# Moving 32 tile transposes from TensorE to the DMA crossbar in a fused attention and MLP kernel

## The chip, the cores and the metric

The kernel runs on one core of one Trainium2 chip. The metric is the device time of one execution in microseconds (us). Most executions of one kernel agree within a per cent or so; a run counts as slow when it is over 1.5% above the fastest of its kernel. The kernel before ran again in every round of experiments (medians 234.05, 234.35, 234.15 and 233.81); the kernel after did not, so an experiment is compared with it by their ratios to the kernel before. Ratios quoted with an interval are the mean time of one kernel's fast runs over the mean of the other's fast runs of the same rounds, with a 95% interval, so they are not quite the ratio of the medians quoted beside them.

Engines: PE is TensorE, PEld its weight loads, DVE is VectorE, ACT is ScalarE, POOL is GpSimd, SP is SyncE, which here does nothing but issue DMAs; "SPq" is SP's DMA queue.

## The reference, cut to what matters

```python
B, S, D, H, F = 1, 2048, 448, 16, 1792        # head size 28, bf16
x  = A_x
xn = layernorm(x)
# branch A: linear attention with a softmax feature map
qkv = xn @ wqkv
phi_q = concat(softmax(q @ w_phi), softmax(-(q @ w_phi)))      # the same for k
o = (phi_q @ (phi_k.T @ v)) / (phi_q @ sum(phi_k) + 1e-6)
A = o @ wo
# branch B: token shift mixer and MLP on xn
x1 = xn + shift(gelu(layernorm(xn) @ w1)) @ w2
B_ = x1 + gelu(layernorm(x1) @ w3) @ w4
return x + A + B_
```

Tokens are cut in 16 tiles of 128. Two of the intermediate results come out with tokens on partitions, but are next needed with features on partitions: the scaled LN2 output `g_tok` (input of `w3`), and the attention output `o_tok` (input of `wo`). Each of these 32 tiles (128 tokens x 448 features, padded to 512) has to be transposed.

## The kernel before

The kernel has a loading and LN1 phase (0 to about 52 us), a k phase (52 to 95 us: k, v, q and the kv sums), and an output phase of four stages of four tiles each (95 us to the end). A helper records all instructions, works out the semaphores, and plays each engine's list in order; that is why most instructions carry the helper's line (L186 matmul, L190 transpose, L194 ACT, L198 elementwise, L201 or L204 DMA) and must be told apart by their tiles.

Buffers are reused under their first name. In the lines of the trace below, `xnT` in the output phase is `oT` and `o_tok`; `phik` there is `h3T` (gelu of the w3 product); `vaug` is the scratch of the attention division, the sums `xs` and the output buffer `outb`; `w` is any of w1, w2, w3, w4; `hi` holds the qk weights at the start, q features later.

The parts that the change and the argument touch:

```python
        def g_apply(i):
            ln_apply(pool, g_tok[:, i % 4, 0:D], xn[:, i, 0:D], rs2, i)

        def g_T(i, b):                                  # LN2 tile, b = banks[7] (banks[5] in the k phase)
            for kc in range(KC):
                R.tr(tview(b)[:, 128 * kc:128 * kc + 128], g_tok[:, i % 4, 128 * kc:128 * kc + 128], ident[:, :])
            j = 128 * (i % 4)
            R.ew(dve, "tensor_copy", gT[:, (i // 4) % 2, :, j:j + 128], tview(b).rearrange("p (c d) -> p c d", c=KC))

        def o_T(i):                                     # attention tile
            b = banks[7]
            for kc in range(KC):
                R.tr(tview(b)[:, 128 * kc:128 * kc + 128], o_tok[:, i % 4, 128 * kc:128 * kc + 128], ident[:, :])
            j = 128 * (i % 4)
            R.ew(dve, "tensor_copy", oT[:, (i // 4) % 2, :, j:j + 128], tview(b).rearrange("p (c d) -> p c d", c=KC))

        def fin_tile(i):
            g, j = divmod(i, 4)
            b = bank(3, 4)
            x_sum(i)                                    # POOL
            # ... 14 matmuls with w4, 4 with wo into b ...
            R.ew(dve, "tensor_tensor", outb[:, i % 4, :], b[:, 0:D], xs[:, i % 2, :], op=ALU.add)
            R.dma(out2d[128 * i:128 * i + 128, :], outb[:, i % 4, :])
# ...
        for g in range(NG):                             # the output phase: 14 w3 chunks per stage,
            fill = []                                   # with this work spread between them
            # ...
            for j in range(4):
                i = 4 * g + j
                fill.append(lambda i=i: num_tile(i))
                if g >= 1:
                    fill.append(lambda i=i - 4: fin_tile(i))
                if g < 2:
                    fill.append(lambda i=i + 8: w2_tile(i))
                    # ...
                if g + 1 < NG:
                    fill.append(lambda i=i + 4: g_T(i, banks[7]))
                if i > 0:
                    fill.append(lambda i=i - 1: o_T(i))
```

Note what is tied together: both transposes of a slot write bank 7, so the second cannot start until DVE has copied the first one out.

The softmax here doesn't subtract the row's maximum and nothing guards it: scores larger than these inputs give would overflow.

Of the kernel before, what the change touches and what calls it, by code (L numbers as in the profile page):

```python
# [17 lines left out]
class Recorder:  # L18
# [177 lines left out]
    def ew(self, eng, name, out, *args, **kw):  # L196
        aps = [v for v in list(args) + list(kw.values()) if hasattr(v, "tensor")]
        self.op(eng, lambda e: getattr(e, name)(out, *args, **kw), [out], aps)  # L198

    def dma(self, out, in_, eng="SP"):  # L200
        self.op(eng, lambda e: e.dma_start(out, in_), [out], [in_], dma=True)  # L201


def bass_parallel_sum__linear_kernel_hedgehog__mixer_s_mlp__prompt_kernel(  # L204
# [6 lines left out]
    NT, NG, KC, NC, NM, FC, HP = 16, 4, 4, 4, 4, 14, 32  # L211
# [6 lines left out]
    with es:  # L218
        R = Recorder(nc, es)
# [9 lines left out]
        def view(h, cols, dt=BF16, at=0):  # L229
            a = h[:, at // 2:at // 2 + cols * DTB[dt] // 2]  # L230
            return a if dt == BF16 else a.bitcast(dt)

        def new(name, cols, dt=BF16):
            return view(region(name, cols * DTB[dt]), cols, dt)

        banks = []
# [16 lines left out]
        gT = new("gT", 2 * KC * 512).rearrange("p (b c s) -> p b c s", b=2, c=KC)  # L253
# [16 lines left out]
        g_tok = new("g_tok", 4 * 512).rearrange("p (b d) -> p b d", b=4)  # L270
        kvq = new("kvq", 8 * 128).rearrange("p (b e) -> p b e", b=8)
        kvT = view(w1_r, NC * 224).rearrange("p (c f) -> p c f", c=NC)
        ident = new("ident", 128)
# [14 lines left out]
        oT = view(xnT_r, 2 * KC * 512).rearrange("p (b c s) -> p b c s", b=2, c=KC)  # L288
        o_tok = view(xnT_r, 4 * 512, at=2 * KC * 512 * 2).rearrange("p (b d) -> p b d", b=4)
# [21 lines left out]
        def bank(*ids):  # L311
            k = turn.get(ids, 0)
            turn[ids] = k + 1
            return banks[ids[k % len(ids)]]

        def tview(b, n=512, base=0):
            return b[:, :].bitcast(BF16)[:, base:base + n]

        dve, pool = "DVE", "POOL"
# [5 lines left out]
        def load_rows(dst, src):  # L325
# [31 lines left out]
                                             fill=0.0, base=0, channel_multiplier=1), [maskb[0:CR, :]], [maskb[0:CR, :]])  # L357
        R.op(pool, lambda e: e.affine_select(mb, mb, pattern=[[DH, 4], [0, DH]], compare_op=ALU.is_ge,
                                             fill=0.0, base=DH - 1, channel_multiplier=-1),
# [4 lines left out]
                                             fill=1.0, base=0, channel_multiplier=1), [rsel[0:DH, :]], [rsel[0:DH, :]])  # L364
# [16 lines left out]
        def ln_scale(mvt, rst, a, n):  # L381
            R.ew(pool, "tensor_scalar", rst[:, a:a + n, 2], mvt[:, a:a + n, 1], LN_EPS, 1.0, op0=ALU.add, op1=ALU.mult)
            R.ew(pool, "tensor_scalar", rst[:, a:a + n, 1], mvt[:, a:a + n, 0], -1.0, 0.0, op0=ALU.mult, op1=ALU.add)
            R.ew(pool, "tensor_tensor", rst[:, a:a + n, 0], rst[:, a:a + n, 2], mhalf[:, 0:n], op=ALU.pow)
# [51 lines left out]
        rot = [(0, 1, 2, 3, 4, 5)]  # L436

        def rot_b():
            return bank(*rot[0])

        def v_tile(i):
            b = rot_b()
            for kc in range(KC):
                R.mm(b[:, 0:D], xnT[:, kc, 128 * i:128 * i + 128], wv[:, kc, :], kc == 0, kc == KC - 1)
            R.ew(dve, "tensor_copy", vaug[:, i, :].rearrange("p (h e) -> p h e", e=HP)[:, :, 0:DH],
                 b[:, 0:D].rearrange("p (h e) -> p h e", e=DH))

        def k_tile(i):
            b = rot_b()
            for kc in range(KC):  # L450
                R.mm(b[:, 0:D], xnT[:, kc, 128 * i:128 * i + 128], wpk[:, kc, :], kc == 0, kc == KC - 1)
            R.act(phik[:, i, 0, :], b[:, 0:D], ACT.Exp)
            R.act(phik[:, i, 1, :], b[:, 0:D], ACT.Exp, scale=-1.0)
            ph = phik[:, i, :, :].rearrange("p s (h e) -> p (s h) e", e=DH)
            r = i % 4
            R.ew(dve, "tensor_reduce", ksum[:, r, :], ph, axis=AX.X, op=ALU.add)
            R.ew(dve, "reciprocal", rks[:, r, :], ksum[:, r, :])
            R.ew(pool, "tensor_tensor", ph, ph, rks[:, r, :].unsqueeze(2).to_broadcast([128, 2 * H, DH]), op=ALU.mult)

        def kv_tile(i):  # L460
            for c in range(NC):
                R.mm(banks[6 + c // 2][:, 224 * (c % 2):224 * (c % 2) + 224].rearrange("p (s f) -> p s f", s=2),
                     vaug[:, i, 128 * c:128 * c + 128], phik[:, i, :, CR * c:CR * c + CR],
                     i == 0 and c % 2 == 0, i == NT - 1)
# [23 lines left out]
        def w2_tile(i):  # L488
            b = rot_b()
            for m in range(NM):  # L490
                c0 = 2 + 128 * i - SHIFTS[m]
                R.mm(b[:, 0:D], hT[0:CR, m, c0:c0 + 128], w2[0:CR, m, :], m == 0, m == NM - 1)
            R.ew(dve, "tensor_tensor", xn[:, i, 0:D], b[:, 0:D], xn[:, i, 0:D], op=ALU.add)
            ln_stats(st2, mv2, xn, i)
# [1 line left out]
        def g_apply(i):  # L496
            ln_apply(pool, g_tok[:, i % 4, 0:D], xn[:, i, 0:D], rs2, i)

        def g_T(i, b):
            for kc in range(KC):  # L500
                R.tr(tview(b)[:, 128 * kc:128 * kc + 128], g_tok[:, i % 4, 128 * kc:128 * kc + 128], ident[:, :])
            j = 128 * (i % 4)
            R.ew(dve, "tensor_copy", gT[:, (i // 4) % 2, :, j:j + 128], tview(b).rearrange("p (c d) -> p c d", c=KC))

        def num_tile(i):
            g, j = divmod(i, 4)
# [17 lines left out]
                 q_n[:, r, :, 0:DH], rden.unsqueeze(2).to_broadcast([128, H, DH]), op=ALU.mult)  # L524

        def o_T(i):
            b = banks[7]
            for kc in range(KC):
                R.tr(tview(b)[:, 128 * kc:128 * kc + 128], o_tok[:, i % 4, 128 * kc:128 * kc + 128], ident[:, :])
            j = 128 * (i % 4)  # L530
            R.ew(dve, "tensor_copy", oT[:, (i // 4) % 2, :, j:j + 128], tview(b).rearrange("p (c d) -> p c d", c=KC))

        def w3_chunk(g, fc):
            b = bank(0, 1, 2)
# [4 lines left out]
        def x_sum(i):  # L539
            R.ew(pool, "tensor_tensor", xs[:, i % 2, :], xn[:, i, 0:D], xtok[:, i, :], op=ALU.add)  # L540

        def fin_tile(i):
            g, j = divmod(i, 4)
            b = bank(3, 4)
            x_sum(i)
            for fc in range(FC):
                R.mm(b[:, 0:D], h3T[:, g % 2, fc, 128 * j:128 * j + 128], w4[:, fc, :], fc == 0, False)
            for kc in range(KC):
                R.mm(b[:, 0:D], oT[:, g % 2, kc, 128 * j:128 * j + 128], wo[:, kc, :], False, kc == KC - 1)
            R.ew(dve, "tensor_tensor", outb[:, i % 4, :], b[:, 0:D], xs[:, i % 2, :], op=ALU.add)  # L550
            R.dma(out2d[128 * i:128 * i + 128, :], outb[:, i % 4, :])


# [30 lines left out]
        for i in range(NT + 2):  # L584
            if i < NT:
                k_tile(i)
            if i >= 2:
                kv_tile(i - 2)
            if i < NT:
                if i % 2 == 0:  # L590
                    v_tile(8 + i // 2)
                else:
                    w2_tile(i // 2)
                    if i % 8 == 7:
                        ln_scale(mv2, rs2, i // 2 - 3, 4)
                q_chunk(*divmod(i, 4))
                if i == 9:
                    for j in range(4):
                        g_apply(j)
                if i >= 12:  # L600
                    g_T(i - 12, banks[5])
                    rot[0] = (0, 1, 2, 3, 4)
        kv_copy()
        R.ew(pool, "memset", o_tok[:, :, D:512], 0.0)
        rot[0] = (3, 4)
        for g in range(NG):
            fill = []
            if g + 1 < NG:
                fill.append(lambda g=g: [g_apply(4 * g + 4 + j) for j in range(4)])
            if g == 0:  # L610
                fill.append(kv_blocks)
            for j in range(4):
                i = 4 * g + j
                fill.append(lambda i=i: num_tile(i))
                if g >= 1:
                    fill.append(lambda i=i - 4: fin_tile(i))
                if g < 2:
                    fill.append(lambda i=i + 8: w2_tile(i))
                    if j == 3:
                        fill.append(lambda i=4 * g + 8: ln_scale(mv2, rs2, i, 4))  # L620
                if g + 1 < NG:
                    fill.append(lambda i=i + 4: g_T(i, banks[7]))
                if i > 0:
                    fill.append(lambda i=i - 1: o_T(i))
            n = 0
            for fc in range(FC):
                w3_chunk(g, fc)
                while n < len(fill) * (fc + 1) // FC:
                    fill[n]()
                    n += 1  # L630
        o_T(NT - 1)
        for i in range(NT - 4, NT):
            fin_tile(i)

        R.emit()

# [27 lines left out]
```

## Time and profile before

| | before |
|---|---|
| time, median of 4 runs | 234.05 us (233.56 to 234.7) |
| span of the profiled run | 231.3 us |
| PE / DVE / ACT / POOL busy | 88% / 55% / 41% / 40% |
| chain that ended last | PE 62%, DVE 20% |

The first part of the page of the kernel before (busy us, share of the span, instructions per engine):

```profile
PE 204.6 (88%) x1289; PEld 115.9 (50%) x1289; DVE 128.1 (55%) x291; ACT 94.8 (41%) x168; POOL 93.1 (40%) x125
```

PE is the engine that everything waits for. So the next question is when PE does not work. The view of waits of the kernel before, PE alone (who waited, for whom; us in total, times, longest; the lines of 1.5, 1.1 and 0.4 us are cut):

```profile
PE bank L190 <- DMA hi<-in_A_wqkv_dram: 8.3, 2, 8.2
PE bank L190 <- DVE gT L198: 5.6, 6, 2.1
PE bank L186 <- POOL phik L198: 3.2, 3, 1.7
PE bank L190 <- ACT xnT L194: 2.9, 3, 1.1
PE bank L190 <- DVE xnT L198: 0.5, 1, 0.5
```

The first line is the load at the start. The second and the last are the transposes of the output phase: 6.1 us in which PE stands before a transpose (L190) until DVE has copied an earlier one out of bank 7.

The timeline of PE in the kernel before, around the longest of these waits (start us, us busy, what, times; in brackets the idle time before):

```profile
104.96 0.39 PE L190 MATMUL bank<-ident,g_tok 128*128 128x128 bf16 x4
107.44 0.40 PE L190 MATMUL bank<-ident,xnT 128*128 128x128 bf16 x4 [2.09 <-DVE gT L198]
107.67 1.85 PE L186 MATMUL bank<-gT,w 128*128 128x512 bf16 x4
109.32 1.06 PE L186 MATMUL bank<-kvq,eq_lo 112*128 112x128 bf16 x8
...
114.69 0.61 PE L186 MATMUL bank<-kvq,eq_lo 112*128 112x128 bf16 x8
115.14 1.03 PE L186 MATMUL bank<-gT,w 128*128 128x512 bf16 x4
```

An attention tile (`xnT`) stood 2.09 us behind the copy of an LN2 tile (`g_tok`). After the wait the same work is slower: a w3 chunk (4 matmuls) takes 1.85 us where it takes 1.03 later. And a tile's four transposes show 0.40 us of busy time, but the next group starts 0.23 us after them (107.44 to 107.67): matmuls overlap, so the slot that a tile really costs PE is 0.225 us, not 0.40.

The table by stretches for the kernel before (stretch, length, PE busy with its count, granted PE clock, DMA share, GB/s) shows what the slowness is:

```profile
106.00:108.00 2.00, 0.56 (x5) 0.93 0.00 0
108.00:110.00 2.00, 2.00 (x11) 0.50 0.00 0
110.00:112.00 2.00, 2.00 (x11) 0.71 0.00 0
```

After the idle stretch the granted clock is about half for some 3 us, which cost this execution 1.7 us. In p1 (below), whose transposes are also on PE, PE stood before the same attention tile for the same 2.09 us, and the chunk after it ran at full speed (timeline of PE of p1):

```profile
109.14 0.40 PE L190 MATMUL bank<-ident,xnT 128*128 128x128 bf16 x4 [2.09 <-DVE gT L198]
109.37 1.03 PE L186 MATMUL bank<-gT,w 128*128 128x512 bf16 x4
```

### The profile page before, as it was taken

Reading aid. Unit: us, or ns where it says so; the run is one execution under the profiler, and the core shown is the slowest. Engines: PE = TensorE matmul, PEld = TensorE weight load, DVE = VectorE, ACT = ScalarE, POOL = GpSimd, SP = SyncE. Lnnn points to the kernel's source line nnn. Section 1 sums busy time; section 2 is a strip of 40 time slices with the busy share of each in tenths; the row PEclk is TensorE's granted clock in tenths of the full one; section 3 lists DMA queues with packets and bytes.
Section 4 is the critical chain, followed back from the end, with each engine's and each line's share of the span. In section 5 each row is a group of like instructions: output and inputs, shape, how many; then the busy total and the mean of one; then the engine's idle time right before and its main releaser. Section 6 shows DMA issues by size and latency. Waiting matters only on the chain.

```text
span 231.3 us, 3260 instructions
## 1 busy us (share of the span) xinstructions
PE 204.6 (88%) x1289; PEld 115.9 (50%) x1289; DVE 128.1 (55%) x291; ACT 94.8 (41%) x168; POOL 93.1 (40%) x125
## 2 busy tenths in 40 slices
PE   0568989798999999696999889989999999999995
PEld 0545555455666566453545445545555455555452
DVE  6389503048888878686765745743643545244211
ACT  2398493695777756641342312323331233322000
POOL 7816600017558965831157033148113312335220
PEclk9988999999999999998899999999999999999999
DMA  6999800000000000000000000000000000000011
GB/s 175 321 262 288 249 5 0 4 0 0 0 3 0 0 0 3 0 0 0 3 0 0 24 20 0 20 23 0 20 23 20 0 20 23 20 16 4 23 40 40
DMA packets 9580, 9.51 MB, mean 41 GB/s; under 512 B 990, under 2 KB 9118, under 8 KB 9566
## 3 DMA queue, kind: packets, MB, share of 16 engines
q1 hardware_dynamic: 9104, 9.29, 14.1%
q8 instruction: 10, 0.16, 0.3%
q10 hardware_dynamic: 462, 0.03, 0.1%
q14 instruction: 4, 0.03, 0.0%
HBM read 7.48 MB, written 1.84 MB: 40 GB/s over the span
## 4 chain that ended last, share of the span: by engine, by line
PE 62%; DVE 20%; POOL 7%; ACT 5%; DMA 3%; issue 2%; SPq 1%; DVEq 0%
PE bank L186 57%; DVE vaug L198 8%; PE bank L190 5%; DVE st L198 5%; POOL phik L198 3%; DMA hi<-in_A_wqkv_dram 3%; DVE xn L198 2%; DVE mv L198 1%; DVE ksum L198 1%; DVE gT L198 1%; POOL vaug L198 1%; POOL xnT L198 1%; POOL g_tok L198 1%; ACT phik L194 1%; ACT hi L194 1%
## 5 line engine op out<-in xcount | busy, mean ns | idle before, releaser
L194 ACT ACTIVATE phik<-bank 128x512 bf16<-128x512 f32 (+1 forms) x88 | 49.1, 580 | 85.9 <-PE bank L186 85.9
L186 PE MATMUL bank<-gT,w 128*128 128x512 bf16 x224 | 57.8, 386 | 0.0
L198 DVE TENSOR_TENSOR vaug<-bank,vaug 128x464 f32<-128x464 f32 (+2 forms) x64 | 33.3, 520 | 38.2 <-POOL vaug L198 25.3
L186 PE MATMUL bank<-w,phik 128*128 128x448 bf16 x224 | 45.0, 352 | 0.0
L198 POOL TENSOR_TENSOR xnT<-vaug 128x448 bf16<-128x448 f32 x16 | 15.1, 941 | 73.8 <-DVE vaug L198 73.8
L198 POOL TENSOR_TENSOR phik<-phik,rks 128x896 bf16<-128x896 bf16 x16 | 27.1, 1697 | 36.3 <-DVE rks L198 36.1
L186 PEld LDWEIGHTS bank<-w,phik 128*128 128x128 bf16 x224 | 21.8, 98 | 20.7
L186 PEld LDWEIGHTS bank<-gT,w 128*128 128x128 bf16 x224 | 20.8, 99 | 18.3 <-issue 1.1
L198 DVE TENSOR_REDUCE ksum<-phik 128x32 f32<-128x896 bf16 x16 | 17.3, 1082 | 18.4 <-ACT phik L194 18.4
L198 POOL TENSOR_TENSOR vaug<-xn,xtok 128x448 f32<-128x448 bf16 x16 | 16.4, 1031 | 6.5 <-DVE vaug L198 6.5
L194 ACT ACTIVATE hi<-bank 112x512 bf16<-112x512 f32 (+1 forms) x20 | 12.4, 680 | 14.9 <-PE bank L186 8.0
L186 PE MATMUL bank<-xnT,w 128*112 128x512 bf16 x64 | 17.0, 407 | 1.5 <-ACT xnT L194 1.5
L186 PE MATMUL bank<-xnT,wpq 128*112 128x512 bf16 x64 | 16.4, 379 | 0.0
L186 PE MATMUL bank<-w,hT 112*128 112x448 bf16 x64 | 14.8, 353 | 0.0
L186 PE MATMUL bank<-wo,xnT 128*128 128x448 bf16 x64 | 14.7, 352 | 0.0
L186 PE MATMUL bank<-wpk,xnT 128*128 128x448 bf16 x64 | 14.7, 352 | 0.0
L198 DVE CAST vaug<-bank 128x448 bf16<-128x448 f32 x16 | 9.5, 593 | 8.6 <-PE bank L186 7.8
L194 ACT ACTIVATE hT<-bank 112x512 bf16<-112x512 f32 x16 | 9.6, 597 | 11.0 <-PE bank L186 10.8
L186 PE MATMUL bank<-wv,xnT 128*128 128x448 bf16 x64 | 13.7, 352 | 0.0
L198 DVE RECIPROCAL vaug<-bank 128x16 f32<-128x16 f32 x16 | 4.1, 257 | 15.2 <-PE bank L186 15.2
L190 PE MATMUL bank<-ident,xnT 128*128 128x128 bf16 x64 | 6.3, 221 | 6.3 <-DVE gT L198 5.6
L186 PE MATMUL bank<-phik,vaug 128*128 128x224 bf16 x64 | 8.8, 259 | 3.2 <-POOL phik L198 3.2
(69 smaller groups left out, 237.3 us busy)
## 6 DMA issues: line engine op xcount, KB each, us to landing
out_dram<-vaug SPq DMA_DIRECT2D x16, 112.0 KB, 1.7
w<-in_B_w_dram SPq DMA_DIRECT2D x1, 1568.0 KB, 17.4
xtok<-in_A_x_dram SPq DMA_DIRECT2D x3, 448.0 KB, 7.6
w<-in_B_w_dram SPq DMA_DIRECT2D x1, 1344.0 KB, 12.7
hi<-in_A_wqkv_dram SPq DMA_DIRECT2D x1, 672.0 KB, 6.3
xtok<-in_A_x_dram SPq DMA_DIRECT2D x2, 224.0 KB, 2.9
w<-in_B_w_dram SPq DMA_DIRECT2D x1, 392.0 KB, 9.0
w<-in_B_w_dram SPq DMA_DIRECT2D x1, 336.0 KB, 6.8
```

What stands on the lines that cost most here:

```text
L186: self.op("PE", lambda e: e.matmul(out, lhsT, rhs, start=start, stop=stop, skip_group_check=True), [out], [lhsT, rhs])
L190: self.op("PE", lambda e: e.transpose(out, in_, ident), [out], [in_, ident])
L194: self.op("ACT", lambda e: e.activation(out, in_, func, **kw), [out], [in_] + aps)
L198: self.op(eng, lambda e: getattr(e, name)(out, *args, **kw), [out], aps)
```

## The change

The intent: take the transposes off the bottleneck engine. A DMA can transpose a tile on its way from SBUF to SBUF (DMA_TRANSPOSE in the traces, a crossbar transpose in this text), and the DMA engines are nearly idle in the output phase (busy share 0.00 to 0.08). PE loses 128 transposes, DVE 32 copies, and bank 7 becomes free for the rotation of the output sums. Because SP issues its DMAs in order (a1 below shows what that costs), a store that waits for its tile would hold up the transposes behind it; so each store is queued one tile later.

```diff
+    def dma_t(self, out, in_, eng="SP"):
+        self.op(eng, lambda e: e.dma_start_transpose(out, in_), [out], [in_], dma=True)
@@ g_T
-        def g_T(i, b):
-            for kc in range(KC):
-                R.tr(tview(b)[:, 128 * kc:128 * kc + 128], g_tok[:, i % 4, 128 * kc:128 * kc + 128], ident[:, :])
+        def g_T(i):
             j = 128 * (i % 4)
-            R.ew(dve, "tensor_copy", gT[:, (i // 4) % 2, :, j:j + 128], tview(b).rearrange("p (c d) -> p c d", c=KC))
+            R.dma_t(gT[:, (i // 4) % 2, :, j:j + 128], g_tok[:, i % 4, :])
@@ o_T: the same, with oT and o_tok (cut)
@@ fin_tile
-            b = bank(3, 4)
+            b = rot_b()
 ...
+        def store(i):
             R.dma(out2d[128 * i:128 * i + 128, :], outb[:, i % 4, :])
@@ k phase
-                    g_T(i - 12, banks[5])
-                    rot[0] = (0, 1, 2, 3, 4)
+                    g_T(i - 12)
@@ output phase
-        rot[0] = (3, 4)
+        rot[0] = (3, 4, 7)
 ...
                 if g >= 1:
+                    if i > 4:
+                        fill.append(lambda i=i - 5: store(i))
                     fill.append(lambda i=i - 4: fin_tile(i))
 ...
         o_T(NT - 1)
+        store(NT - 5)
         for i in range(NT - 4, NT):
             fin_tile(i)
+            store(i)
```

More of the change, by code (lines that the diff above doesn't have):

```diff
@@ L526, in o_T @@
         def o_T(i):
-            b = banks[7]
-            for kc in range(KC):
-                R.tr(tview(b)[:, 128 * kc:128 * kc + 128], o_tok[:, i % 4, 128 * kc:128 * kc + 128], ident[:, :])
             j = 128 * (i % 4)
-            R.ew(dve, "tensor_copy", oT[:, (i // 4) % 2, :, j:j + 128], tview(b).rearrange("p (c d) -> p c d", c=KC))
+            R.dma_t(oT[:, (i // 4) % 2, :, j:j + 128], o_tok[:, i % 4, :])
         def w3_chunk(g, fc):
@@ L621, in bass_parallel_sum__linear_kernel_hedgehog__mixer_s_mlp__prompt_kernel @@
                 if g + 1 < NG:
-                    fill.append(lambda i=i + 4: g_T(i, banks[7]))
+                    fill.append(lambda i=i + 4: g_T(i))
                 if i > 0:
```

## The prediction

> **What bounds the kernel now.** TensorE is 88% busy over the 231.3 us span, DVE 55% (first part of the page); the chain that ended last is 62% PE, 20% DVE. By stage, PE is busy 29.2 of 30.0 us in 142 to 172 us and 30.4 of 31.0 in 172 to 203: PE-bound. In the first output stage (95 to 121 us) PE and DVE take turns: PE 19.8, DVE 17.0 of 22.8 us, PE clock 0.93.
>
> **Removed.** 32 tile transposes on PE (4 matmuls of 128x128 each) and 32 DVE copies (424 and 403 ns, 13.3 us). The 0.39 us of PE busy time per tile overstates the cost: in the timeline the next group starts 0.225 us after a tile's first transpose. So 28 tiles of the output phase cost 6.3 us, the 4 in the k phase 0.9 (I count 0.5, as PE is not alone in limiting there). Waiting costs as much: both transposes share bank 7, so the second waits for the DVE copy of the first, which stands in DVE's queue behind other work. The waits show PE idle 5.6 us for the gT copy and 0.5 for the oT copy, in stalls of 0.5, 0.8 and 2.1 us. After the 2.1 us stall at 105 us the clock drops: 4 matmuls took 1.85 us instead of 1.03, and two more groups ran slow, 1.7 us in all.
> By output stage: first 6 us, second 4.5, third 2.7, fourth 1.4, k phase 0.5: about 15 us, nearly all critical.
>
> **Added.** 32 crossbar transposes of 128x512 bf16 (128 KB) on the SP queue, which there has only 16 stores. A 112 KB store takes 0.33 us on the queue and lands in 1.7 us. The Trainium skill (Advanced Engine Details and Errata, X-Bar Transpose) says transposes are as fast as regular DMAs; DMA: Bandwidth & Descriptors (Latency and other measured facts) gives 261 GB/s in the unfavourable case, 0.5 us of data. I estimate 2 to 4 us to landing and 1 us of queue time; no run here shows it yet. DMA engines are idle in this phase (share 0.00 to 0.08).
>
> **Is it hidden?** oT is read a whole stage later. gT is needed at the next stage's first w3 chunk; its last transpose sits in SP's in-order queue behind a store that waits for the previous tile's DVE sum. That store is released about 2 us after that tile's matmuls, and 7 us of PE work follow: 2 to 4 us fit, with little to spare. I allow 1 to 2 us for new waits at stage boundaries and for num_tile's banks (5 and 6, not doubled; DVE needs 2.3 us to free them). DVE then needs 3.7 us of each 4.2 us slot in the first stage, so it should just keep up.
>
> **Predicted:** 220.5 us (6% faster), 8 in 10 between 215 and 227. Chances: faster by over 2% 0.86, within 2% 0.08, slower 0.06.
>
> **What would show it.** Right: no idle PE before transposes, no DVE copies of gT and oT, PE clock 1.0 after 100 us, stages two and three shorter by 4.5 and 2.7 us, PE idle before w3 chunks under 1 us per boundary, transposes landing in under 4 us. Wrong: PE or POOL waiting for DMA into gT, oT or out of g_tok, o_tok; SP busy most of a stage.
>
> **What would make it wrong.** A transpose that takes over 4 us and runs strictly one after another: the first stage needs seven within 20 us and would wait, as would the stores behind. Or the first stage turning out DVE-bound through num_tile's banks, giving back its 6 us.

## The result, and the profile after

| | before | after |
|---|---|---|
| time, median of 4 runs | 234.05 us (233.56 to 234.7) | 218.88 us (217.17 to 220.07) |
| ratio of the fast runs | | 0.9345 [0.9267, 0.9423] |
| span of the profiled run | 231.3 us | 215.1 us |
| chain that ended last, share of PE | 62% | 77% |

The time fell by 6.5%. The first part of the page of the kernel after:

```profile
PE 194.1 (90%) x1161; PEld 108.2 (50%) x1161; DVE 115.5 (54%) x259; ACT 94.9 (44%) x168; POOL 93.2 (43%) x125
```

PE has 128 instructions less (1289 to 1161), DVE 32 less (291 to 259). The view of waits of the kernel after, PE alone:

```profile
PE bank L190 <- DMA hi<-in_A_wqkv_dram: 8.4, 1, 8.4
PE bank L186 <- POOL phik L198: 3.7, 3, 2.2
PE bank L190 <- ACT xnT L194: 2.9, 3, 1.1
PE bank L186 <- ACT xnT L194: 1.4, 2, 0.8
PE bank L190 <- POOL rs L198: 1.0, 1, 1.0
PE bank L186 <- DVE kvq L198: 0.4, 1, 0.4
```

The two lines of transposes waiting for DVE are gone, and no line has come in their place: none names a DMA into gT or oT. The timeline of PE after, over the same stretch of work as the one shown of before:

```profile
101.94 1.03 PE L186 MATMUL bank<-gT,w 128*128 128x512 bf16 x4
102.80 0.92 PE L186 MATMUL bank<-w,hT 112*128 112x448 bf16 x4
103.56 1.89 PE L186 MATMUL bank<-gT,w 128*128 128x512 bf16 x8
105.29 0.61 PE L186 MATMUL bank<-kvq,eq_lo 112*128 112x128 bf16 x8
105.74 1.03 PE L186 MATMUL bank<-gT,w 128*128 128x512 bf16 x4
```

There is no bracket, so no idle time, and every w3 chunk runs at full speed (two in 1.89 us).

Where the 16.2 us of span went, by the start of the same group of work in both timelines:

| from, to | before | after | saved |
|---|---|---|---|
| first attention tile of stage 1 to that of stage 2 | 98.85 to 121.36 | 98.55 to 114.62 | 6.4 |
| stage 2 to stage 3 | 121.36 to 156.80 | 114.62 to 145.17 | 4.9 |
| stage 3 to stage 4 | 156.80 to 187.07 | 145.17 to 171.82 | 3.6 |
| stage 4 to the output sum of tile 12 | 187.07 to 214.66 | 171.82 to 198.46 | 1.0 |
| before and after that | | | 0.3 |

The kernel after runs one w3 chunk (0.86 us) less in stage 3 and one more in stage 4; with that put right the two stages save 2.8 and 1.8 us. The sum can be redone from the timeline of the kernel before: 28 slots of 0.225 us (6.3), the seven waits with the hidden 0.165 us each (7.3; the bracket counts idle time only from the end of the 0.39 us), three stalls too short for a bracket (0.6), the slow clock (1.7) and 0.3 at the start make 16.2 us.

The new cost is on SP's queue. The DMA part of the view of DMA issues after (out, in, queue, how often, median us from issue to landing):

```profile
gT<-g_tok SPq DMA_TRANSPOSE x16, 2.5
xnT<-xnT SPq DMA_TRANSPOSE x16, 2.5
```

And the timeline of SP after, one slot of stage 2 and the next store:

```profile
134.77 0.33 SPq L204 DMA_DIRECT2D out_dram<-vaug  x1
135.14 1.19 SPq L201 DMA_TRANSPOSE gT<-g_tok  x1
136.38 1.27 SPq L201 DMA_TRANSPOSE xnT<-xnT  x1
141.98 0.33 SPq L204 DMA_DIRECT2D out_dram<-vaug  x1
```

A transpose holds the queue for 1.2 us, a store for 0.33; together they fill 2.8 of the about 7 us that a tile's turn in stage 2 takes. The transposes add 17,400 DMA packets (9,580 before, 26,987 after) and 4.2 MB, and the busy share of the DMA engines in the output phase rises from 0.08 at most to 0.16 to 0.28. Three of the 32, all of attention tiles, landed only after 4.1 to 4.3 us; nothing waited for them. The LN2 tile issued at 135.14 is the last that stage 3 needs; it lands at about 137.6, and stage 3's first w3 chunk starts at about 143.4: the transposes are hidden with 5.8 us to spare. At the next boundary the last is issued at 164.88 and lands at about 167.4, and the chunk starts at about 171.0: 3.6 us to spare. The boundary into stage 2 is the tightest: the last is issued at 107.36 and lands at about 109.9, and the chunk starts at about 112.9, 3.0 us later. (The starts of the chunks are the second or third of a merged group, with 0.86 us for each chunk before.)

### The profile page after: what moved, and what is told of

Read it like the earlier page. It is cut to its first block, busy times and chain, and to the rows that moved or that the text cites. A ratio compares the mean times of both kernels' runs of the same rounds, so it can differ in the third digit from the quotient of the medians.

```text
span 215.1 us, 3027 instructions
## 1 busy us (share of the span) xinstructions
PE 194.1 (90%) x1161; PEld 108.2 (50%) x1161; DVE 115.5 (54%) x259; ACT 94.9 (44%) x168; POOL 93.2 (43%) x125
## 2 busy tenths in 40 slices
DMA packets 26987, 13.70 MB, mean 64 GB/s; under 512 B 18398, under 2 KB 26526, under 8 KB 26974
## 4 chain that ended last, share of the span: by engine, by line
PE 77%; DVE 7%; ACT 5%; POOL 5%; DMA 3%; issue 1%; SPq 0%
PE bank L186 74%; POOL phik L198 3%; DMA hi<-in_A_wqkv_dram 3%; DVE st L198 3%; PE bank L190 3%; DVE ksum L198 2%; POOL g_tok L198 1%; ACT phik L194 1%; DVE mv L198 1%; ACT hi L194 1%; ACT xnT L194 1%; ACT hT L194 1%; ACT L194 1%; DVE kvq L198 1%; DVE rks L198 1%
## 5 line engine op out<-in xcount | busy, mean ns | idle before, releaser
L186 PE MATMUL bank<-gT,w 128*128 128x512 bf16 x224 | 53.9, 379 | 0.0
L186 PE MATMUL bank<-w,phik 128*128 128x448 bf16 x224 | 45.0, 352 | 0.0
L186 PEld LDWEIGHTS bank<-w,phik 128*128 128x128 bf16 x224 | 21.9, 98 | 20.9
L186 PEld LDWEIGHTS bank<-gT,w 128*128 128x128 bf16 x224 | 21.2, 98 | 21.6
L186 PE MATMUL bank<-xnT,w 128*112 128x512 bf16 x64 | 17.0, 407 | 1.4 <-ACT xnT L194 1.4
L186 PE MATMUL bank<-xnT,wpq 128*112 128x512 bf16 x64 | 16.4, 379 | 0.0
L186 PE MATMUL bank<-w,hT 112*128 112x448 bf16 x64 | 14.8, 353 | 0.0
L186 PE MATMUL bank<-wo,xnT 128*128 128x448 bf16 x64 | 14.7, 352 | 0.0
L186 PE MATMUL bank<-wpk,xnT 128*128 128x448 bf16 x64 | 14.7, 352 | 0.0
L186 PE MATMUL bank<-wv,xnT 128*128 128x448 bf16 x64 | 13.7, 352 | 0.0
L186 PE MATMUL bank<-phik,vaug 128*128 128x224 bf16 x64 | 8.8, 259 | 3.7 <-POOL phik L198 3.7
L190 PE MATMUL bank<-ident,hi 128*112 128x128 bf16 x32 | 3.8, 312 | 8.5 <-DMA hi<-in_A_wqkv_dram 8.4
```

What stands on the lines that cost most here:

```text
L186: self.op("PE", lambda e: e.matmul(out, lhsT, rhs, start=start, stop=stop, skip_group_check=True), [out], [lhsT, rhs])
L190: self.op("PE", lambda e: e.transpose(out, in_, ident), [out], [in_, ident])
```

## The experiments

The theory: the gain has two halves of nearly the same size: PE's slots for the transposes, and PE's waits that come from two transposes sharing one bank behind a busy DVE; the crossbar itself is hidden. Rivals: the regrouped stores and banks carry the gain; the gain is proportional to the tiles moved; the waits would only have moved elsewhere.

### p1: the later stores and the bank rotation alone

```diff
 (from the kernel after)
-            R.dma_t(gT[...], g_tok[:, i % 4, :])
+            b = banks[5 if i < 4 else 7]                # PE transposes and DVE copy, as before
+            # ...
-            R.dma_t(oT[...], o_tok[:, i % 4, :])
+            b = banks[7]                                # as before
+            # ...
-        rot[0] = (3, 4, 7)
+        rot[0] = (3, 4)
 (the k phase's rot[0] = (0, 1, 2, 3, 4) comes back too; cut)
```

> Both transposes back on TensorE in bank 7 with their DVE copies; only the later stores and the shared bank rotation (3 and 4) of the change remain. Theory (the gain comes from taking the transposes off PE and from the waits in bank 7): nothing gained, 233 to 235 us, and PE still idle about 6 us for the gT and oT copies. Rival (the later stores or the merged rotation carry a good part of the gain): 229 us or less.

Measured: 234.47 us against 234.35, ratio 1.002 [0.996, 1.008]; PE waits 6.6 us for gT copies and 0.8 for oT copies. The later stores bring nothing by themselves. The rival that gave them a part of the gain falls. The third bank for the output sums, (3, 4, 7), was never run alone; but neither the kernel before nor p2 nor p3, all with two banks, shows PE waiting for a bank of these sums.

### p2 and p3: one of the two kinds of tile alone

p2 sends only `g_tok` through the crossbar, p3 only `o_tok`; the other kind stays on PE with bank 7 to itself (for LN2 tiles of the k phase bank 5).

```diff
 (from the kernel after; p2)
-            R.dma_t(oT[...], o_tok[:, i % 4, :])
+            b = banks[7]                                # PE transposes and DVE copy, as before
 (p3)
-            R.dma_t(gT[...], g_tok[:, i % 4, :])
+            b = banks[5 if i < 4 else 7]                # PE transposes and DVE copy, as before
 (the k phase's rot[0] comes back as in p1; cut)
 (both)
-        rot[0] = (3, 4, 7)
+        rot[0] = (3, 4)
```

> Only the LN2 tiles go through the crossbar; attention tiles stay on TensorE, alone in bank 7. Theory: the wait in bank 7 needs two users of the bank, so all of its 6 us and the 1.7 us of slow clock go, with the PE slots of 16 tiles (3.5 us): about 223 us. Rival (each tile moved is worth the same, half of 15 us for half of the tiles): about 226.5 us.

> Only the attention tiles go through the crossbar; LN2 tiles stay on TensorE, alone in bank 7 (bank 5 in the k phase). Theory: as with the other half alone, waits gone and 16 PE slots saved, about 223 us. Rival (each tile is worth the same): about 226.5 us.

Measured: p2 224.00 us, ratio 0.953 [0.947, 0.960]; p3 224.06 us, ratio 0.957 [0.952, 0.962]. Half of the tiles gives 10.3 us of the 15.2 (medians), two thirds: whichever half moves, most of the waiting goes with it. Proportionality would have given about 226.5 us, or a ratio of 0.967, which lies outside both intervals. p2 keeps one wait, of an attention tile for the copy of the attention tile before it (0.8 us, once). p3 keeps a rest of waiting, but of a new kind, in its view of waits for PE:

```profile
PE bank L186 <- DVE gT L198: 2.3, 3, 1.0
```

That is not a transpose (L190) but the w3 chunk itself (L186), at the start of a stage, waiting for DVE to copy the last LN2 tile out.

### p4: no crossbar, but two banks

The cheapest alternative: the kernel before, with bank 2 given to the attention tiles.

```diff
 (from the kernel before)
         def o_T(i):
-            b = banks[7]
+            b = banks[2]
         def w3_chunk(g, fc):
-            b = bank(0, 1, 2)
+            b = bank(0, 1)
```

> The kernel before with no crossbar transposes; the attention transposes get bank 2 for themselves, the w3 chunks rotate over two banks instead of three. Theory: the waits and the slow clock after them go, the PE slots stay: about 226.5 us, PE idle for the gT copy near 0. Rival (DVE is late anyway, or the third w3 bank was needed, so waiting only moves): 232 us or more.

Measured: 227.67 us against 234.35, ratio 0.971 [0.966, 0.976]. The waits of transposes for gT copies are gone. The time is 1.2 us above the expected 226.5; new waits of 1.8 us at the stage boundaries can account for that. The timeline of PE of p4:

```profile
116.41 0.39 PE L190 MATMUL bank<-ident,xnT 128*128 128x128 bf16 x4
117.74 1.90 PE L186 MATMUL bank<-gT,w 128*128 128x512 bf16 x8 [0.95 <-DVE gT L198]
```

Now both transposes go back to back, but the first chunk of the next stage stands 0.95 us for the copy of the last tile. In all PE waits 1.8 us for gT there, and 0.5 for an oT copy. So about 6.7 us of the 15.2 us had nothing to do with the crossbar: one more PSUM bank would have bought them. The other 8.5 us (227.67 less the 218.88 of the kernel after, with the 0.3 us between the two medians of the kernel before) needed the transposes off PE: 7.2 us of slots (32 times 0.225) and 2.3 us of waits for DVE's copies are 9.5 by the trace; the 1 us of difference is within the intervals of the two ratios.

### a1: the stores back at their own tile

```diff
 (from the kernel after)
-                    if i > 4:
-                        fill.append(lambda i=i - 5: store(i))
-                    fill.append(lambda i=i - 4: fin_tile(i))
+                    fill.append(lambda i=i - 4: (fin_tile(i), store(i)))
 ...
-        store(NT - 5)
```

> The changed kernel with each output store queued right after its own tile again. The last gT transpose of a stage then stands behind a store that waits for the DVE sum of the last tile. Theory (the later store is what keeps the transposes of gT ahead of the stage boundary): the sum comes about 2 us after that tile's matmuls, the transpose needs 2.5 us more, and only 1 to 2 us of PE work lie between, so PE waits 2 to 3 us at each of the two boundaries into stages three and four: 222 to 225 us. Rival (there is room enough, the later store is idle decoration): 218 to 220 us, no PE wait at the boundaries.

Measured: 224.98 us, ratio 0.961 [0.957, 0.966]: 6 us of the gain are lost. The timeline of SP of this run at the last slot of stage 3, and then of PE:

```profile
175.11 0.33 SPq L204 DMA_DIRECT2D out_dram<-vaug  x1
175.49 1.19 SPq L201 DMA_TRANSPOSE gT<-g_tok  x1
```

```profile
145.19 1.03 PE L186 MATMUL bank<-gT,w 128*128 128x512 bf16 x4
147.47 1.89 PE L186 MATMUL bank<-gT,w 128*128 128x512 bf16 x8 [1.25 <-ACT phik L194]
...
174.11 1.03 PE L186 MATMUL bank<-gT,w 128*128 128x512 bf16 x4
178.05 3.51 PE L186 MATMUL bank<-gT,w 128*128 128x512 bf16 x8 [2.91 <-DMA gT<-g_tok]
```

The transpose stands behind the store, the store behind DVE's sum; issued at 175.49 it lands 2.5 us later, and PE starts at 178.05. At the boundary before (147.47) the profile names ACT, but the transpose was issued at 144.96 in that run, and 144.96 plus 2.5 is 147.46: so it is most likely the same wait, put down to another semaphore of the same instruction. The waits are 4.2 us together, and after the longer one two chunks took 3.51 us instead of 1.89. So the small edit that brings nothing alone (p1) is worth 6 us beside the crossbar: with the transposes on PE nothing but stores was in that queue.

### a2: twice as many transposes of half the size

```diff
 (from the kernel after)
     def dma_t(self, out, in_, eng="SP"):
-        self.op(eng, lambda e: e.dma_start_transpose(out, in_), [out], [in_], dma=True)
+        for c in (0, 2):
+            self.half_t(out[:, c:c + 2, :], in_[:, 128 * c:128 * c + 256], eng)
+
+    def half_t(self, out, in_, eng):
+        self.op(eng, lambda e: e.dma_start_transpose(out, in_), [out], [in_], dma=True)
```

> The changed kernel with each crossbar transpose split into two of half the columns, the same bytes in twice the instructions. Theory (the transposes are hidden): the same time, 217 to 221 us, PE never waiting for gT. What it measures: if the cost is per instruction, a half takes about 1.2 us on the queue and 2.4 us to land; if per byte, 0.6 us on the queue and about 1.8 us to land.

Measured: 218.62 us over all four runs; the ratio, without the one that was counted as slow, is 0.932 [0.927, 0.937], the same as the kernel after. PE waited for gT once, 0.5 us, at the start of stage 2, the tightest boundary. A half-size transpose holds the queue for 1.24 us and lands after 2.4: at these widths the cost is per instruction. The theory that the crossbar is hidden stands even with twice the queue time.

### a8: what a transpose costs by its width

```diff
 (from the kernel after, at the end)
             fin_tile(i)
             store(i)
+        gflat = g_tok.rearrange("p b d -> p (b d)")
+        scr = view(hi_r, 2048).rearrange("p (c s) -> p c s", s=128)      # dead by then
+        for n in (1, 2, 4, 8, 16, 1, 2, 4, 8, 16):
+            R.dma_t(scr[:, 0:n, :], gflat[:, 0:128 * n])
```

> A measurement, not a contest: after the last store, ten more transposes into a dead buffer, one after another, each waiting for the one before, of 128x128, 256, 512, 1024 and 2048, twice. Outputs stay right; the time grows by about 30 us. If the cost is per instruction, queue time stays near 1.2 us and landing near 2.4 us up to 512 columns, and rises above that only when the data (512 KB at the widest) takes longer; if per byte, 2048 columns take four times as long as 512.

Measured once (244.72 us, state unknown, which does not matter for single DMAs). The timeline of SP of this run, the second series, 128, 256, 512, 1024 and 2048 columns of 128 rows:

```profile
228.00 1.12 SPq L201 DMA_TRANSPOSE hi<-g_tok  x1
230.28 1.18 SPq L201 DMA_TRANSPOSE hi<-g_tok  x1
232.57 1.19 SPq L201 DMA_TRANSPOSE hi<-g_tok  x1
235.00 1.23 SPq L201 DMA_TRANSPOSE hi<-g_tok  x1
238.09 1.92 SPq L201 DMA_TRANSPOSE hi<-g_tok  x1
```

| columns | 128 | 256 | 512 | 1024 | 2048 |
|---|---|---|---|---|---|
| us on the queue | 1.12 | 1.18 | 1.19 | 1.23 | 1.92 |
| us from issue to landing | 2.3 | 2.3 | 2.4 | 3.1 | 4.4 |

Each starts when the one before has landed. Sixteen times the data takes 1.9 times as long to land. The tiles of this kernel sit on the flat part. The first series agrees within 0.1 us.

### a3 and a5: the LN1 tiles through the crossbar too

There are 16 more transposes before the k phase (`xn_T`, PE and an ACT copy of 0.6 us each), and PE waits for these copies (2.9 us in the view of waits above, plus 1.4 for the chunk after them).

```diff
 (from the kernel after; a3 with 4, a5 with 8)
         def xn_T(i):
+            if i >= 4:
+                R.dma_t(xnT[:, :, 128 * i:128 * i + 128], xn[:, i, :])
+                return
             b = bank(0, 1)
```

> An attempt to beat it: the LN1 tiles 4 to 15 go through the crossbar as well, instead of 48 TensorE transposes and 12 ACT copies of 0.6 us. If that stage (24 to 52 us) is limited by PE and by the ACT copies it waits for: 2.7 us of PE slots and about 3 us of waits saved, 213 to 216 us. Rival (the transposes queue behind the weight loads and each other at 1.25 us per tile, so the first w1 chunks wait for xnT): no gain or a loss, 219 us or more.

Measured: 219.87 us, ratio 0.941 [0.935, 0.946]: no gain. The view of waits for PE of a3, and its timeline after that wait:

```profile
PE bank L186 <- DMA xnT<-xn: 7.7, 1, 7.7
```

```profile
32.53 1.93 PE L186 MATMUL bank<-xnT,w 128*112 128x512 bf16 x4 [7.68 <-DMA xnT<-xn]
34.25 0.58 PE L186 MATMUL bank<-bd,hi 112*128 112x112 bf16 x4
34.62 1.92 PE L186 MATMUL bank<-xnT,w 128*112 128x512 bf16 x4
```

Tiles 4 to 7 are needed at once when they are ready, while the weight loads are still running, so nothing hides their way through the queue. And the DMA engines are full with the loads (busy share about 1 until 26 us): the first of these transposes held the queue for 3.1 us and landed after 8.8, the next three after 6.2, 4.7 and 2.5. After the 7.7 us of idle PE the clock is half (1.93 us for what takes 1.03). Later tiles have time (in a5 the first landed after 5.4 us, and nothing waited for it). So a5 leaves tiles 4 to 7 on PE:

> A second attempt at the LN1 tiles: only tiles 8 to 15 go through the crossbar, whose source is ready after the weight loads have landed; tiles 4 to 7 stay on TensorE. Theory (the first attempt lost its gain to one 7.7 us wait for the first transposes, issued while the loads still ran, and to the slow clock after it): no wait for xnT over 1 us, 8 PE tiles (1.8 us) and two or three ACT-copy waits of 0.8 to 1.1 us saved, 213 to 216 us. Rival (the crossbar is no gain in that stage at all): 218 us or more.

Measured: 213.09 us against 233.81, ratio 0.910 [0.906, 0.913]. PE's wait for ACT's xnT copies before its transposes falls to 2.0 us and before chunks to 0.7, and no DMA into xnT appears in the waits. This beats both kernels.

### a4: the first LN2 scalings on DVE

```diff
 (from the kernel after)
         def g_apply(i):
-            ln_apply(pool, g_tok[:, i % 4, 0:D], xn[:, i, 0:D], rs2, i)
+            ln_apply(dve if i < 4 else pool, g_tok[:, i % 4, 0:D], xn[:, i, 0:D], rs2, i)
```

> Another attempt: the first four LN2 scalings (g_tok) move from POOL (0.72 us each) to DVE (about 0.4 us each), in the k phase, where PE waits 3.7 us for POOL's phik. If POOL is what limits there: 2 to 3.5 us saved, 215 to 217 us, PE waiting for phik under 1 us. Rival (DVE is about as full there and now delays the ksum that POOL needs): 218 us or more.

Measured: 218.68 us, ratio 0.935 [0.930, 0.941]: no gain, as the rival expected. The wait for POOL's phik stays at 3.4 us, and its longest, 2.2 us at the end of the k phase, did not move. POOL was itself waiting for DVE there (its last phik starts 1.06 us after it fell idle, in both kernels): that wait is the latency of a chain from the last k tile through ACT, DVE and POOL, not POOL's load. Taking other work off POOL did not shorten it; other work for PE could cover it.

### a6 and a7: work for PE during that latency, and both gains together

```diff
 (from the kernel after; a7 has the edit of a5 as well)
             if i >= 2:
+                if i == NT + 1:
+                    w3_chunk(0, 0)
+                    w3_chunk(0, 1)
                 kv_tile(i - 2)
 ...
-            for fc in range(FC):
+            f0 = 2 if g == 0 else 0
+            for fc in range(f0, FC):
                 w3_chunk(g, fc)
-                while n < len(fill) * (fc + 1) // FC:
+                while n < len(fill) * (fc - f0 + 1) // (FC - f0):
```

> The changed kernel with two w3 chunks of the first output stage moved ahead of the last kv tile, where PE waits 2.2 us for the chain ACT, DVE, POOL of the last k tile; their operand gT lands 4 us earlier than that. If that wait is pure latency: PE works through it, 216 to 217.5 us (2 us less). Rival (kv_copy and kv_blocks now wait, or ACT changes its function table earlier): no gain, 218 us or more.

Measured: 216.81 us, ratio 0.927 [0.923, 0.931]. The timeline of PE of a6:

```profile
94.28 1.67 PE L186 MATMUL bank<-gT,w 128*128 128x512 bf16 x7
96.41 0.56 PE L186 MATMUL bank<-phik,vaug 128*128 128x224 bf16 x4 [0.45 <-POOL phik L198]
...
100.36 0.62 PE L186 MATMUL bank<-kvq,eq_lo 112*128 112x128 bf16 x8 [1.22 <-DVE kvq L198]
```

The wait of 2.2 us becomes 0.45, but the wait for kvq grows from 0.4 to 1.2, since there is less w3 work left to cover it. The 2 us between the medians of this and the kernel after are as expected, but the two intervals overlap, so the size of this gain is not settled.

> The two edits before together. If both gains are on the PE chain they add up: 211.5 to 214 us, 9 to 10% under the kernel before.

Measured: 212.17 us (211.27 to 212.34, 5 runs) against 233.81, ratio 0.905 [0.901, 0.909]: the fastest version found, 9.5% under the kernel before. Over a5 that is about 1 us, with intervals that overlap; the two gains add up at most in part.

## Why the prediction was right

It forecast 220.5 us (215 to 227) and the median was 218.88. Point by point:

- "Both transposes share bank 7, so the second waits for the DVE copy of the first": shown. PE's waits before these transposes are gone after the change, p2 and p3 remove them by leaving one kind of tile in the bank, and p4 by a second bank.
- The half that is waiting (forecast: 6.1 us of idle PE and 1.7 us of slow clock) and the half that is PE slots (6.3 us in the output phase): p4 gives 6.7 us for the first, already less 1.8 us of new waits, and the rest of the gain for the second. The size of the waiting half, 7.8 us, was right partly by luck. The 1.7 us of slow clock were put down to the wait, which p1 does not bear out; and the mean granted clock of the four runs of the kernel after (0.992, 0.992, 0.976, 0.992) is no better than that of the kernel before in the other rounds (0.984 to 1.0). In its place stand the parts of the waits that the view does not show: by the pitch of the timeline the waits and short stalls cost 7.9 us, not 6.1. Taking the pitch between groups (0.225 us) instead of the busy time (0.39 us) for the slot was right: with 0.39 the slots would have been 12.5 us, and half and half would not fit p4.
- By stage: 6, 4.5, 2.7 and 1.4 forecast; 6.4, 4.9, and with equal chunks 2.8 and 1.8 measured in the profiled runs, the first with 1.7 us of slow clock in it. The 0.5 us of the k phase did not come as such: PE's wait for POOL's phik there grew from 3.2 to 3.7 us, and the work before the first attention tile is 0.3 us shorter.
- "2 to 4 us to landing and 1 us of queue time": 2.5 and 1.2 us in the median, 4.1 to 4.3 us to landing for three of the 32. "2 to 4 us fit, with little to spare": 3.0, 5.8 and 3.6 us were left at the three boundaries. The 1 to 2 us that were allowed for new waits never came: no wait for a DMA or for the attention banks shows after the change. That allowance is a term that was mis-sized, and it is about the size of the 1.6 us by which the forecast was too high.
- "its last transpose sits in SP's in-order queue behind a store": a1 shows how close that was. With the store one tile earlier the same queue costs 6 us.
- "the first stage needs seven [transposes] within 20 us and would wait": it did not; a2 doubled their number and stayed as fast.
- Of the things that could make it wrong, none came. What the prediction took from the Trainium skill (Advanced Engine Details and Errata, X-Bar Transpose (TRN2): a transpose is as fast as a regular DMA; DMA: Bandwidth & Descriptors, Latency and other measured facts: 261 GB/s) was of little use for the size: it is the fixed cost that counts here (a8).

What stays open: why the runs of the kernel after spread by 1.3% (217.2 to 220.1), and what brings the granted clock down. After the 2.2 us wait at the end of the k phase the clock was halved in the profiled runs of a4 and a5 and not in those of the kernel after, p2, a1, a2 and a3. Such a drop does not explain the whole spread: the fastest run of the kernel after and the slowest have the same mean clock, 0.992.

## What to carry to other kernels

When the bottleneck engine waits for two users of one buffer, count the waits and the work apart: here a second PSUM bank alone was worth 6.7 us, and moving the work away another 8.5. A crossbar transpose of a 128x512 tile costs 1.2 us of an in-order queue and mostly 2.5 us to land, and a narrower one hardly less (a8), so it is free where the result is needed several us later and the queue is not blocked by a DMA that waits for something else; where the consumer is already waiting and the DMA engines are busy with loads (a3) it loses. Before queueing such a DMA, look at what stands in front of it.

## What the Trainium skill lacked or had wrong

- DMA: Bandwidth & Descriptors, Latency and other measured facts, gives a transpose by bandwidth alone (261 GB/s, or 350 to 400). (One 128x128 tile has a time elsewhere in the skill; how the time to landing goes with the width was found on no page.) For SBUF to SBUF tiles the fixed cost decides: 2.3 us to landing for 128 columns (32 KB), 2.4 for 512 (128 KB, so about 55 GB/s), 3.1 for 1024, 4.4 for 2048. The step from 1024 to 2048 columns (256 KB more in 1.3 us) gives an estimate of about 200 GB/s for the data itself.
- Advanced Engine Details and Errata, X-Bar Transpose (TRN2), says that transposes are as fast as regular DMAs. Here a 128 KB transpose held the issuing queue for 1.2 us and landed after 2.5, while a 112 KB store (to DRAM, not to SBUF) held it for 0.33 us and landed after 1.7. Neither of the two sections has the queue time of a transpose, which is what limits how many fit in a stage, nor what loads in flight do to it (8.8 us to landing in a3).
- TensorE: Matmul & The Clock Gate, Why this matters for your kernels, asks for no idle gaps over about 3 us. Here idle gaps of 2.1 us (kernel before) and 2.2 us (a4, a5) were followed by a granted clock of about 0.5 to 0.6 for some 3 to 4 us; the same 2.2 us gap in the profiled run of the kernel after was not, nor was the same 2.1 us gap in p1. The length of the gap alone does not decide it here.
- The same page, PE-mode transpose, gives about 275 ns for a 128x128 transpose in a kernel. The trace shows 219 ns of duration, but a pitch of 56 ns (four in 0.225 us); the pitch is what a PE-bound kernel gains by removing one.
